# Block sums moved from GpSimd to VectorE, and every engine's steps ordered by one written table

## The chip, the core and the metric

The kernel runs on one core of a Trainium2 chip. The core has a matrix unit (TensorE: PE, its weight loads PEld), VectorE (DVE), ScalarE (ACT), GpSimd (POOL), and SyncE (SP), which here only issues DMA transfers. Each engine works through its own list of instructions in order; semaphores tie the lists together, so an instruction that waits holds up all that stands behind it on its engine. The metric is device time in microseconds (us); lower is better.

## What is computed

A decayed linear attention (2 batches, 8 heads, 768 positions, 64 features) feeds two expert layers with 1536 tokens, width 512 and inner width 2048:

```
for t in range(S):
    state = gamma * state + outer(k[t], v[t])        # per batch and head
    y[t] = scale * q[t] @ state
x = y as (1536, 512)
h = x @ moe_w_in;   x = elu(h) @ moe_w_out           # first layer
h = x @ moe2_w_in;  out = softplus(h) @ moe2_w_out   # second layer
```

The weights arrive as 64-bit floats. They are put together on chip from their two 32-bit halves. Products are made at higher than single-pass precision: each operand is split into a high and a low part, and three products (high·high, high·low, low·high) are added.

## The kernel before

**Stages.** The first stage runs attention (12 tiles of 128 positions) beside the first layer. The layer is worked in 48 units: 3 blocks of 512 tokens by 16 slices of the inner width. For unit u, `H.u` (`hidden`, L432, 12 matmuls) makes the hidden values, `aa`/`ab` apply the activation, `gh`/`gl` split it into high and low parts, and `R.u` (`project`, L470, 12 matmuls) adds into four output banks. `ih`/`il` and `oh`/`ol` split the two weight tiles of the unit. The third block of tokens is units 32 to 47.

The second stage is the second layer as 16 "quads": 2 groups of 768 tokens by 8 slices of the inner width. Its first product uses a scheme with seven block products (`multiply`, L613, numbers 1 to 7 of `products`, 6 matmuls each) in place of eight, at the price of sums and differences of operand blocks. For the weights these are `combine_w` (L544, four GpSimd operations on 128x256 in a quad of the first group, three in one of the second). For the tokens they are `combine_x` (L522, four GpSimd operations on 128x768 per group). `block_h/l` (L564, L567), `sum_h/l` (L575, L578), `operand_h/l` (L527, L532) and `out_h/l` (L582, L586) split the results. Products 1, 6, 7, 4 accumulate in one bank and 2, 5, 3 in another. ScalarE copies the partial results out of the first bank (`keep`, L620) before the next product may enter it. `gather` (L632, on VectorE, or L630 on ScalarE), `negate` (L636), `soften` (L640), `join` (L644), `gate_h` (L650) and `gate_l` (L654) make the gated values, and `project2` (L670, four times 9 matmuls per quad) multiplies them by the second weights.

**Weight conversion.** 64 weight tiles are loaded, 512 KB each, into four rotating `raw` buffers (L188, on SP's queue; for the first 32 loads every fifth goes to a spare buffer). A tile is converted by two ScalarE operations (L197, L198) and two VectorE operations (L210, L211). The second layer's tiles overwrite those of the first, and so can be converted only when the third block of tokens has used them.

**What sets the order.** The pools and semaphores are fixed, and the order in which the program calls its steps is the order on each engine. Three things make that order: `OPENING`, a written list of steps for the first third; `regular()`, a rule that goes on from there to the last units; and `quad()`, which gives every step of the second stage a due time, by which all are sorted. At the end of the first stage `regular()` has left several tiles of the second layer unconverted, and `quad()` puts two conversions into each of the first quads:

```python
        for n, (a1, b1) in enumerate(((3.8, 4.5), (9.9, 11.0))):
            if todo:
                i = todo.pop(0)
                at(t + a1, conv_a, i)
                at(t + b1, conv_b, i)
```

The tokens' operands of the second group are made at the end of the first group, by steps with due times from the start of the last quad of the first group on.

Of the kernel before, what the change touches and what calls it, by code (L numbers as in the profile page):

```python
# [11 lines left out]
F32 = mybir.dt.float32  # L12
F32R = mybir.dt.float32r
# [25 lines left out]
def tile_retention_elu_softplus(  # L39
# [134 lines left out]
    raws = {}  # L174
    parts = {}
    wide64 = w_in1.dtype != F32

    def load_w(i):
# [3 lines left out]
        if not wide64:  # L182
            nc.sync.dma_start(out=wf[f][o], in_=src)
            return
        spare = i < 2 * NF and i % 5 == 4
# [104 lines left out]
    def transposed(n, j):  # L290
        if j in blocked:
# [4 lines left out]
            if n == 0:  # L296
                nc.gpsimd.tensor_tensor(out=tf, in0=tf, in1=gq[j >= CPB], op=ALU.mult)
# [10 lines left out]
        elif j in plain:  # L308
# [3 lines left out]
        qkT[n, j] = t  # L312

# [6 lines left out]
    def state(j):  # L320
# [6 lines left out]
        else:  # L327
            tag = f"h{1 - max(hb) % 2}"
# [90 lines left out]
    hb = {}  # L419
    gs_ = {}  # L420
# [3 lines left out]
    def hidden(u):  # L424
# [31 lines left out]
    def project(u):  # L456
        layer, blk, f = units[u]
        oh, ol = ws.pop((u, 1))
        gh, gl = gs_.pop(u)
        fresh = f == 0  # L460
        if fresh:
            for i in range(4):
                acc[i] = psum(f"a{i}")
# [4 lines left out]
        for p, i in order:  # L468
# [19 lines left out]
    def finish(u):  # L488
        _, blk, f = units[u]
        if f != NF - 1:  # L490
            return
        for i in range(4):
            t = blk * TB
            parts = []
            while t < (blk + 1) * TB:
                e = min((blk + 1) * TB, (t // HT + 1) * HT)
                parts.append((t, e))
                t = e
            for n, (t, e) in enumerate(sorted(parts, key=lambda x: x[0] - x[1])):
                h = t // HT  # L500
                dst = yhalf(h // 2, h % 2)[:, i, t - h * HT:e - h * HT]
                src = acc[i][:, t - blk * TB:e - blk * TB]
                if n == 0:
                    nc.scalar.activation(out=dst, in_=src, func=AF.Copy)
                else:
                    nc.vector.tensor_copy(dst, src)
# [6 lines left out]
    source = (0, 2, 0, 0, 1, 2, 3)  # L513
# [453 lines left out]
```

## Time and profile before

| | us |
|---|---|
| median of 3 runs | 598.24 (597.95 to 600.91) |
| profiled execution, its own time | 596.96 |
| its span, first to last instruction | 595.2 |
| PE busy | 574.4 (97%) |
| VectorE busy | 458.9 (77%) |
| ScalarE busy | 377.3 (63%) |
| GpSimd busy | 100.8 (17%) |

PE's busy time is not PE at its peak, since matmuls overlap and their ends are modelled. The spacing from one matmul's start to the next says more. Of the other engines only the moments matter in which PE waits for them.

### The profile page before, as it was taken

Reading aid. Unit: us, or ns where it says so; the run is one execution under the profiler, and the core shown is the slowest. Engines: PE = TensorE matmul, PEld = TensorE weight load, DVE = VectorE, ACT = ScalarE, POOL = GpSimd, SP = SyncE. Lnnn points to the kernel's source line nnn. Section 1 sums busy time; section 2 is a strip of 40 time slices with the busy share of each in tenths; the row PEclk is TensorE's granted clock in tenths of the full one; section 3 lists DMA queues with packets and bytes.
Section 4 is the critical chain, followed back from the end, with each engine's and each line's share of the span. In section 5 each row is a group of like instructions: output and inputs, shape, how many; then the busy total and the mean of one; then the engine's idle time right before and its main releaser. Section 6 shows DMA issues by size and latency. Waiting matters only on the chain.

```text
span 595.2 us, 8756 instructions
## 1 busy us (share of the span) xinstructions
PE 574.4 (97%) x3236; PEld 487.5 (82%) x3236; DVE 458.9 (77%) x729; ACT 377.3 (63%) x678; POOL 100.8 (17%) x101
## 2 busy tenths in 40 slices
PE   8999899999999999999999799999996999999996
PEld 5888688888888888888888688889885999889995
DVE  3899899976555647899998798888789876766653
ACT  2596887946454456987997666666664655555542
POOL 3310200010010000215002222222225111111000
PEclk9999999999999999999999799999998999999999
DMA  9985958753220002233434122200000200000002
GB/s 198 275 272 158 259 171 210 196 134 60 38 47 9 1 1 72 71 107 106 143 108 140 35 72 71 72 0 2 1 0 1 107 1 1 1 0 2 1 0 106
DMA packets 75835, 48.30 MB, mean 81 GB/s; under 512 B 53520, under 2 KB 69904, under 8 KB 75792
## 3 DMA queue, kind: packets, MB, share of 16 engines
q1 hardware_dynamic: 75216, 46.94, 28.7%
q10 hardware_dynamic: 576, 0.80, 0.4%
q8 instruction: 25, 0.41, 0.3%
q14 instruction: 18, 0.15, 0.1%
HBM read 44.58 MB, written 3.15 MB: 80 GB/s over the span
## 4 chain that ended last, share of the span: by engine, by line
PE 70%; DVE 13%; issue 7%; ACT 4%; SPq 4%; DMA 2%; POOL 1%; ACTq 0%; DVEq 0%; POOLq 0%
PE psb L470 21%; PE psb L432 19%; PE psb L670 14%; PE psb L613 13%; SPq L97 3%; DVE cl L210 2%; DVE wo L586 2%; DMA v<-v 1%; DVE hx L632 1%; DVE g L654 1%; DVE hx L644 1%; PE psb L353 1%; DVE wo L211 1%; DVE op L532 1%; ACT g L650 1%
## 5 line engine op out<-in xcount | busy, mean ns | idle before, releaser
L670 PE MATMUL psb<-wo,g 128*128 128x512 f32 x576 | 142.9, 393 | 0.0
L670 PEld LDWEIGHTS psb<-wo,g 128*128 128x128 f32 x576 | 108.2, 189 | 19.6
L432 PE MATMUL psb<-x,wh 128*128 128x512 f32 x384 | 95.9, 391 | 0.0
L432 PEld LDWEIGHTS psb<-x,wh 128*128 128x128 f32 x384 | 71.5, 188 | 15.2 <-issue 0.3
L544 POOL TENSOR_TENSOR y<-wi 128x256 f32<-128x256 f32 x48 | 49.6, 1053 | 196.5 <-DVE wx L578 117.8
L613 PE MATMUL psb<-op,wx 128*128 128x384 f32 x336 | 68.7, 344 | 3.4 <-DVE hx L632 2.3
L613 PEld LDWEIGHTS psb<-op,wx 128*128 128x128 f32 x336 | 61.3, 192 | 7.0 <-DVE hx L632 2.8
L640 ACT ACTIVATE hx<-hx 128x384 f32<-128x384 f32 x64 | 33.6, 524 | 44.6 <-DVE hx L636 44.5
L470 PE MATMUL psb<-gh,wh 128*128 128x512 f32 x192 | 56.0, 398 | 0.0
L470 PE MATMUL psb<-gh,wl 128*128 128x512 f32 x192 | 54.4, 390 | 0.0
L470 PE MATMUL psb<-gl,wh 128*128 128x512 f32 x192 | 54.3, 389 | 0.0
L210 DVE SCALAR_TENSOR_TENSOR cl<-cm,cl 128x512 int32<-128x512 int32 x64 | 48.6, 759 | 5.3 <-ACT cl L198 5.3
L650 ACT ACTIVATE g<-hx 128x384 fp32r<-128x384 f32 x64 | 33.4, 523 | 29.9 <-DVE hx L644 29.9
L432 PE MATMUL psb<-x,wl 128*128 128x512 f32 x192 | 51.3, 389 | 0.0
L654 DVE TENSOR_TENSOR g<-hx,g 128x384 fp32r<-128x384 f32 x64 | 37.1, 581 | 16.7 <-ACT g L650 16.4
L439 ACT ACTIVATE e<-psb 128x512 f32<-128x512 f32 x48 | 28.4, 592 | 32.4 <-PE psb L432 31.3
L224 DVE TENSOR_TENSOR wl<-wo,wh 128x512 fp32r<-128x512 f32 x48 | 35.0, 729 | 17.9 <-ACT wh L218 17.8
L644 DVE SCALAR_TENSOR_TENSOR hx<-hx 128x384 f32<-128x384 f32 x64 | 37.3, 584 | 14.7 <-ACT hx L640 12.9
L197 ACT ACTIVATE cm<-raw 128x512 f32<-128x512 f32 x64 | 42.4, 662 | 7.7 <-DMA raw<-moe_w_out 3.7
L613 PE MATMUL psb<-op,wa 128*128 128x384 f32 x192 | 39.8, 349 | 6.5 <-ACT hx L630 2.4
L444 DVE SCALAR_TENSOR_TENSOR e<-e,psb 128x512 f32<-128x512 f32 x48 | 32.6, 680 | 16.8 <-ACT e L440 16.8
L613 PEld LDWEIGHTS psb<-op,wa 128*128 128x128 f32 x192 | 34.9, 193 | 10.4 <-ACT hx L630 4.1
(98 smaller groups left out, 933.1 us busy)
## 6 DMA issues: line engine op xcount, KB each, us to landing
raw<-moe_w_in SPq DMA_DIRECT2D x32, 512.0 KB, 4.0
raw<-moe_w_out SPq DMA_DIRECT2D x32, 512.0 KB, 3.6
out_dram<-o SPq DMA_DIRECT2D x9, 256.0 KB, 2.4
early<-q SPq DMA_DIRECT2D x4, 256.0 KB, 4.9
early<-k SPq DMA_DIRECT2D x4, 256.0 KB, 5.1
early_v<-v SPq DMA_DIRECT2D x4, 256.0 KB, 5.0
qb<-q SPq DMA_DIRECT2D x64, 16.0 KB, 2.2
qb<-k SPq DMA_DIRECT2D x64, 16.0 KB, 1.9
```

The lines of the kernel that those rows point to most:

```text
L197: nc.scalar.activation(out=m, in_=r[:, :, :, 1].bitcast(F32), func=AF.Copy, scale=2.0 ** -112)
L210: nc.vector.scalar_tensor_tensor(out=l, in0=m.bitcast(I32), scalar=3, in1=l, op0=ALU.logical_shift_left, op1=ALU.bitwise_or)
L224: nc.vector.tensor_tensor(out=l, in0=wf[f][o], in1=ws[u, o][0].bitcast(F32), op=ALU.subtract)
L432: nc.tensor.matmul(b, w[:, kk, :], x[:, kk, :], start=(n == 0), stop=(n == len(seq) - 1))
L470: nc.tensor.matmul(acc[i], st[:, i * P:(i + 1) * P], mv, start=(fresh and p == 0), stop=(f == NF - 1 and p == 2))
L544: nc.gpsimd.tensor_tensor(out=out, in0=x, in1=y, op=o)
L613: nc.tensor.matmul(bank_p[b], w[:, h, k], x[:, l, k], start=(start and i == 0), stop=(i == len(seq) - 1), skip_group_check=True)
L640: nc.scalar.activation(out=e, in_=e, func=AF.Softplus)
L644: nc.vector.scalar_tensor_tensor(out=e, in0=h, scalar=0.0, in1=e, op0=ALU.max, op1=ALU.add)
L650: nc.scalar.activation(out=t[:, 0], in_=hid[Q, c][1], func=AF.Copy)
L654: nc.vector.tensor_tensor(out=t[:, 1], in0=hid.pop((Q, c))[1], in1=t[:, 0].bitcast(F32), op=ALU.subtract)
L670: nc.tensor.matmul(sums2[s], t[:, x, i * P:(i + 1) * P], o[:, w], start=(left[s] == 0 and p == 0), stop=(left[s] == 2 * NQ - 1 and p == 2) ...
```

## The change

`combine_w` and `combine_x` run on VectorE. In the second group two of the three weight sums become one operation on 128x512. A spare tile `t2` takes one of the four token differences, so that it overwrites nothing. The operands 0 and 1 of the second group go into the `raw` buffers, which are free by then, and can so be made while the first group still uses its own. Conversion is cut into four steps (`ct`, `cl` on ScalarE, `cj`, `cs` on VectorE), the activation into `ar` and `ae`, the copies of the first layer's result into eight steps `F`, and `project` can be called for part of its matmuls. `OPENING`, `regular()` and `quad()` are gone: `TABLE` lists every step. The number of matmuls does not change. Output tiles come from `tmp` rather than `raw`, and all but one are sent from SP's queue.

```diff
-    def combine_x(n):
-        g, n = divmod(n, 8)
-        d, a, b = ((0, 1, 0), (1, 3, 1), (0, 3, 0), (2, 2, 0))[n]
-        nc.gpsimd.tensor_tensor(out=quarter(g, d), in0=quarter(g, a), in1=quarter(g, b), op=ALU.subtract)
+        second["t2"] = second["op"].tile([P, KK // 2 * HT], F32, name="t2")
+
+    def combine_x(g, n):
+        d, a, b = ((0, 1, 0), (1, 3, 1), (4, 3, 0), (2, 2, 4))[n]
+        nc.vector.tensor_tensor(out=place(g, d), in0=place(g, a), in1=place(g, b), op=ALU.subtract)
+
+    def operand_h(g, n):
+        if g and n < 2:
+            t = [raw.tile([P, 4 * 2 * P], F32R, tag="raw", name=f"op{n}")[:, :KK // 2 * HT] for i in range(2)]
...
-    def combine_w(Q):
+    def combine_w(Q, n):
         a, s = quads(Q), sums()
-
-        def op(out, x, y, o):
-            nc.gpsimd.tensor_tensor(out=out, in0=x, in1=y, op=o)
-
         if Q < NQ:
...
+            out, x, y = ((s[:, 0], a[:, 2], a[:, 3]), (s[:, 2], a[:, 0], a[:, 2]), (a[:, 2], s[:, 0], a[:, 0]),
+                         (s[:, 1], a[:, 1], a[:, 2]))[n]
+        elif n < 2:
+            out, x, y = ((s[:, 0], a[:, 2], a[:, 0]),
+                         (s[:, 1:3], a[:, 1::2], a[:, 2:3].to_broadcast([P, 2, KH])))[n]
...
+        nc.vector.tensor_tensor(out=out, in0=x, in1=y, op=ALU.subtract if n else ALU.add)
...
-PAUSE = {7: 2, 8: 1, 9: 1, 10: 1}
-OPENING = """
...
+TABLE = """
...
+gl.39 ct.46 cs.44 R.38 ar.40 cj.45 Lw.48 ih.42 cs.45 ae.40 il.42 cl.46 Lw.49 ab.40 ct.47 H.41 oh.40 cj.46 gh.40 ol.40 cl.47
+gl.40 ct.48 cj.47 R.39 cs.46 ar.41 cs.47 ih.43 Lw.50 ae.41 Lw.51 il.43 cl.48 ab.41 ct.49 cj.48 H.42 gh.41 cs.48 oh.41 cl.49
...
+    for t in TABLE.split():
+        name, *args = t.split(".")
+        steps[name](*map(int, args))
```

Three places show how instructions move. Line numbers are those of the kernel that each list belongs to. The first is ScalarE's list where the two stages meet. Before, from the second `keep` of quad 0 (first row) to the third `keep` (seventh row):

```order
L620 ACTIVATE hx<-psb 128x384
L504 ACTIVATE y_2620<-psb 128x384 x4
L650 ACTIVATE g_3458<-hx 128x384
L575 ACTIVATE wb<-y_2620 128x768
L197 ACTIVATE cm<-raw 128x512
L198 ACTIVATE cl<-raw 128x512
L620 ACTIVATE hx<-psb 128x384
L582 ACTIVATE wo_3469<-wo_124 128x512
```

After, from the same second `keep` (L703 is `keep`, L585 the copy of the first layer's result, L658 `sum_h`, L665 `out_h`, L731 `gate_h`):

```order
L703 ACTIVATE hx<-psb 128x384
L585 ACTIVATE y_2565<-psb 128x384 x3
L703 ACTIVATE hx<-psb 128x384
L665 ACTIVATE wo_3538<-wo_124 128x512
L731 ACTIVATE g_3548<-hx 128x384
L658 ACTIVATE wb<-y_2565 128x768
```

The third `keep` now stands behind three copies; four other operations that stood ahead of it, among them a conversion, are gone or stand behind it.

The second place is VectorE's list there. Before, from the first `gate_l` (L654) to the `gather` of the second column (L632):

```order
L654 TENSOR_TENSOR g_3458<-hx,g_3458 128x384
L578 TENSOR_TENSOR wb<-y_2620,wb 128x768
L586 TENSOR_TENSOR wo_3469<-wo_124,wo_3469 128x512
L210 SCALAR_TENSOR_TENSOR cl<-cm,cl 128x512
L211 SCALAR_TENSOR_TENSOR wo_133<-raw,cl 128x512
L632 TENSOR_TENSOR hx<-psb,hx 128x384
L636 TENSOR_SCALAR hx<-hx 128x384
```

After (L293 is the last conversion step, L587 the copies of the first layer's result, L713 `gather`, L669 `out_l`, L735 `gate_l`):

```order
L293 SCALAR_TENSOR_TENSOR wo_139<-raw,cl 128x512
L587 COPY y_2565<-psb 128x128 x4
L713 TENSOR_TENSOR hx<-psb,hx 128x384
L669 TENSOR_TENSOR wo_3538<-wo_124,wo_3538 128x512
L735 TENSOR_TENSOR g_3548<-hx,g_3548 128x384
```

The `gather` now stands ahead of `out_l` and `gate_l`, and the last conversion of the whole program ahead of the copies.

The third place is the meeting of the two groups. Before, GpSimd had these block sums there (L544 weights, L522 tokens):

```order
L544 TENSOR_TENSOR y_2620<-wi_116 128x256 x3
L522 TENSOR_TENSOR y_2620<-y_2620 128x768 x3
L544 TENSOR_TENSOR y_2620<-wi_117 128x256 x3
L522 TENSOR_TENSOR y_2620<-y_2620 128x768
L544 TENSOR_TENSOR y_2620<-wi_118 128x256 x3
```

After, these are rows of VectorE, much earlier, among the gating steps of quads 1 and 2 (L637 `combine_w`, L606 `combine_x`, L619 `operand_l` of the second group):

```order
L637 TENSOR_TENSOR wi_120<-y_2565,wi_120 128x256
L619 TENSOR_TENSOR op_3619<-y_2565,op_3618 128x768
L669 TENSOR_TENSOR wo_3788<-wo_129,wo_3788 128x512
L637 TENSOR_TENSOR y_2565<-wi_120 128x256
L713 TENSOR_TENSOR hx<-psb,hx 128x384
L606 TENSOR_TENSOR y_2565<-y_2565 128x768
L717 TENSOR_SCALAR hx<-hx 128x384
L606 TENSOR_TENSOR t_2391<-y_2565 128x768
```

The token differences of the second group and its first two operands have moved some five quads forward and to another engine; GpSimd has nothing left in the second stage.

## Rows read from the trace of the kernel before

**Rows 1.** Waits of the matrix unit: us in total, times, longest.

```profile
PE psb L390 <- POOL wide L318: 2.4, 1, 2.4
```

**Rows 2.** Matrix unit in order of time, where the stages meet: start, us, what.

```profile
326.43 1.21 PE L613 MATMUL psb<-op,wx 128*128 128x384 f32 x6
329.81 1.99 PE L613 MATMUL psb<-op,wa 128*128 128x384 f32 x6 [2.17 <-ACT hx L620]
334.08 4.76 PE L613 MATMUL psb<-op,wx 128*128 128x384 f32 x18 [2.29 <-DVE hx L632]
338.68 2.23 PE L670 MATMUL psb<-wo,g 128*128 128x512 f32 x9
```

**Rows 3.** The chain that ended last: start, us, what.

```profile
308.73 2.72 PE psb L470 x12
...
344.00 1.14 DVE wa L567
...
409.93 1.13 DVE wa L567
...
466.46 2.07 PE psb L670 x9
...
560.60 2.07 PE psb L670 x9
562.67 2.11 PE psb L613 x12
```

**Rows 4.** Matrix unit in order of time, where the groups meet.

```profile
445.58 1.22 PE L613 MATMUL psb<-op,wx 128*128 128x384 f32 x6
448.19 1.33 PE L613 MATMUL psb<-op,wb 128*128 128x384 f32 x6 [1.40 <-DVE hx L632]
449.35 2.25 PE L670 MATMUL psb<-wo,g 128*128 128x512 f32 x9
452.99 1.32 PE L613 MATMUL psb<-op,wa 128*128 128x384 f32 x6 [1.39 <-ACT hx L630]
456.29 2.14 PE L613 MATMUL psb<-op,wa 128*128 128x384 f32 x6 [1.98 <-DVE hx L632]
458.23 3.01 PE L670 MATMUL psb<-wo,g 128*128 128x512 f32 x9
```

**Rows 5.** VectorE in order of time, where the groups meet.

```profile
430.38 0.56 DVE L644 SCALAR_TENSOR_TENSOR hx<-hx 128x384 f32<-128x384 f32 x1 [0.59 <-ACT hx L640]
...
438.72 1.87 DVE L644 SCALAR_TENSOR_TENSOR hx<-hx 128x384 f32<-128x384 f32 x1 [0.46 <-ACT hx L640]
```

**Rows 6.** VectorE in order of time, where the stages meet.

```profile
311.87 0.68 DVE L210 SCALAR_TENSOR_TENSOR cl<-cm,cl 128x512 int32<-128x512 int32 x1
312.59 0.69 DVE L211 SCALAR_TENSOR_TENSOR wi<-raw,cl 128x512 int32<-128x512 int32 x1
313.20 0.69 DVE L224 TENSOR_TENSOR wl<-wo,wh 128x512 fp32r<-128x512 f32 x1
313.80 0.69 DVE L453 TENSOR_TENSOR gl<-e,gh 128x512 fp32r<-128x512 f32 x1
...
331.22 1.21 DVE L210 SCALAR_TENSOR_TENSOR cl<-cm,cl 128x512 int32<-128x512 int32 x1
```

**Rows 7.** Busy time by stretch: PE, PEld, DVE, ACT, POOL, clock, DMA share, GB/s.

```profile
229.00:316.00 87.00, 87.00 (x385) 72.06 (x384) 77.69 (x112) 72.88 (x129) 13.00 (x8) 1.00 0.35 113
...
344.00:418.00 74.00, 72.19 (x353) 63.48 (x351) 64.45 (x103) 46.48 (x88) 20.61 (x20) 1.00 0.14 43
```

**Rows 8.** Groups by line: busy us, mean ns.

```profile
L345 DVE TENSOR_TENSOR st<-st,dec 128x256 f32<-128x256 f32 x8 | 3.4, 424 | 0.3
```

**Rows 9.** Conversion operation L198 by stretch: ACT busy (count), clock, DMA share, GB/s.

```profile
60.00:75.00 15.00, 3.94 (x6) 1.00 0.91 262
...
300.00:315.00 15.00, 2.67 (x4) 1.00 0.44 140
```

**Rows 10.** DMA issues by tile: KB each, median us to landing.

```profile
raw<-moe_w_in SPq DMA_DIRECT2D x32, 512.0 KB, 4.0
```

More of the change, by code (lines that the diff above doesn't have):

```diff
@@ L181, in load_w @@
         src = src[f * P:(f + 1) * P, :] if o else src[:, f * P:(f + 1) * P].rearrange("(k p) f -> p k f", p=P)
[L182 to L185, printed above, removed]
+        spare = len(loaded) < 2 * NF and len(loaded) % 5 == 4
+        loaded.append(i)
         r = (ap if spare else raw).tile([P, 4, P, 2], I32, tag="raw", name="raw")
@@ L327, in state @@
         else:
-            tag = f"h{1 - max(hb) % 2}"
+            tag = f"h{1 - last[0] % 2}"
             b = bank["s", j] = psum(tag)
@@ L419, in tile_retention_elu_softplus @@
     hb = {}
+    last = [0]
     gs_ = {}
@@ L467, in project @@
             order = [(p, i) for i in range(4) for p in range(3)]
-        for p, i in order:
+        for p, i in order[a:e]:
             st, mv = passes[p]
@@ L486, in yhalf, with finish @@
         return ytile(g)[:, n * KK * HT:(n + 1) * KK * HT].rearrange("p (k t) -> p k t", k=KK)
[L488 to L506, printed above, removed]
+    def finish(u, i, n):
+        blk = units[u][1]
+        a = blk * TB
+        m = (a // HT + 1) * HT
+        t, e = sorted(((a, m), (m, a + TB)), key=lambda x: x[0] - x[1])[n]
+        h = t // HT
+        dst = yhalf(h // 2, h % 2)[:, i, t - h * HT:e - h * HT]
+        src = acc[i][:, t - a:e - a]
+        if n == 0:
+            nc.scalar.activation(out=dst, in_=src, func=AF.Copy)
+        else:
+            nc.vector.tensor_copy(dst, src)
     def quarter(g, n):
@@ L512, in tile_retention_elu_softplus, with place @@
     second = {}
-    source = (0, 2, 0, 0, 1, 2, 3)
+    source = (0, 2, 4, 0, 1, 2, 3)
+    def place(g, n):
+        return second["t2"] if n == 4 else quarter(g, n)
     def close_attention():
@@ L673, in project2 @@
             seen2[g, s] = left[s] + 1
+    outs = {}
     def store(g, s):
-        o = raw.tile([P, 2 * DM], F32, tag="raw", name="o")[:, :DM]
+        o = outs[g, s] = tmp.tile([P, DM], F32, tag=("cm", "cl")[s % 2], name="o")
         if s % 2:
@@ L922, in tile_retention_elu_softplus @@
-    for _, _, fn, args in sorted(plan, key=lambda x: x[:2]):
-        fn(*args)
+        "H": hidden, "ar": act_r, "ae": act_e, "ab": act_b, "gh": act_h, "gl": act_l, "R": project, "F": finish,
+        "kc": keep_clock, "few": few_banks, "end": close_attention,
+        "xt": combine_x, "yh": operand_h, "yl": operand_l, "cw": combine_w, "bh": block_h, "bl": block_l, "sh": sum_h,
+        "sl": sum_l, "wh": out_h, "wl": out_l, "op": open_products, "cf": close_first, "M": multiply, "u": keep, "c": gather,
```

404 lines of the change are left out of this document (133 added, 271 removed).

## The prediction

> **What bounds the kernel now.** I read the busy times first, and then the matrix unit (PE) in order of time against its own pace. Undisturbed, 12 matmuls of a first-layer unit step take 2.72 us, 12 of a block product pair 2.11 and 9 of a projection 2.07 [rows 3], so one matmul costs 0.227, 0.176 and 0.230 us, and one unit (`H` and `R`) 5.44 us. Over the third block of tokens PE has no wait at all: busy 87.00 of 87 us [rows 7]. So PE bounds the kernel, and only what PE loses to others can be won without fewer matmuls. It loses time in four places.
>
> Where the stages meet, from 326.43 to 338.68 us (12.25 us) PE runs 6+6+18 block product matmuls [rows 2], worth 30 × 0.176 = 5.3 us. It loses 7.0 us. The waits name ScalarE's `keep` (L620) and VectorE's `gather` (L632).
>
> Where the groups meet, from 445.58 to 458.23 (12.65 us) it runs 24 block product and 9 projection matmuls [rows 4], worth 4.2 + 2.1 = 6.3 us, and loses 6.4 us. The nine matmuls that follow take 3.01 us where the same nine took 2.25 at 449.35, another 0.8. Together 7.1 us.
>
> In the first quads one step of VectorE (L567) starts at 344.00 and, four quads on, at 409.93 [rows 3]: 16.48 us a quad. Late in the kernel the same projection starts at 466.46 and six quads on at 560.60: 15.69. Each of four quads loses 0.79, 3.2 us in all.
>
> In the opening PE waits once for GpSimd's spreading of the attention state, 2.4 us [rows 1].
>
> These make 7.0 + 7.1 + 3.2 + 2.4 = 19.7 us, the most that a better order can win without touching the matmuls, the start or the tail.
>
> **The change part by part.** GpSimd's block sums. While GpSimd works on SBUF, VectorE's instructions grow: the conversion step L210 takes 0.68 us at 311.87 and 1.21 at 331.22 [rows 6], and `join` (L644) takes 0.56 at 430.38 and 1.87 at 438.72, where the token differences run [rows 5]. The two long stalls of PE sit in such stretches. With GpSimd idle in the second stage all of that stretching goes. What comes in is four operations on 128x256 in a quad of the first group, and one on 128x256 plus one on 128x512 in the second. The same shape from SBUF takes 0.42 us [rows 8], a 128x512 one starts 0.60 after its neighbour [rows 6]: 1.7 and about 1.0 us a quad, and 0.9 us (an estimate by columns from the same rows) for each of eight token differences. In a converting quad VectorE was busy 64.45 of 74 us, 87% [rows 7], its conversions included. Those go, so no quad gets fuller by the sums alone.
>
> Conversions. By the order, 12 stand on VectorE behind the first `gather` before, and none after quad 0 now. They go into the third block of tokens, where the table joins 26 tiles over the eleven units from `H.37` to the first product, 59.8 us of PE. VectorE has there 44 split and activation operations and 51 conversion operations (26 joins, 25 signs). At 0.605 us from start to start, as the back-to-back rows stand [rows 6], these are 57.5 us; at their full 0.69 us, 65.6. So VectorE is between 2 us under PE and 6 over. I take 1.5 us lost, near the spacing, because the table puts other work between the two dependent conversion steps, and because VectorE was busy 77.69 of 87 us in this block [rows 7] while PE lost nothing.
>
> Where the stages meet, PE's own order is nearly the old one: `R.47` is only cut into 9 and 3 matmuls, with a block product between. What moved is ahead of it. The third `keep` stood behind four copies, a gate, a sum and a conversion on ScalarE, and now stands behind three copies; the `gather` stood behind a conversion on VectorE and now does not. `keep` can start when product 7 ends, and the three matmuls of `R.47` cover it (0.68 us). I keep back 0.7 us; the bounds are 0 and the 2.2 us that the wait has now [rows 2].
>
> Quads 1 and 2 take the token differences and two operands of the second group. By the order a quad of the first group holds 15 gating steps on 384 columns (at most 0.48 us each by columns, an estimate from the 0.60 for 512 [rows 6]; four of them are lighter, so some 6.5), `block_l` 1.14 [rows 3], one more sum of 768 columns 0.9, two weight splits 1.2 and the block sums 1.4 to 1.7: 11.3. Quad 2 adds three token differences and two operands of 768 columns, 0.9 each: 15.8 of PE's 15.69, and quad 1 about as much, since the last column of quad 0 falls into it. Bounds: 0, and twice what a converting quad loses now, 2 × 1.6 = 3.2 us. I take 1.0. This is the steepest load of the second stage; from quad 3 on it is 13 us and less.
>
> Where the groups meet nothing runs on GpSimd, and the operands 0 and 1 are there long before; 2 to 6 are made as their tiles come free. I keep back 0.8 us; the bounds are 0 and one wait of 1.4 [rows 4].
>
> The opening. The value tile of attention step 5 and its decay come ahead of their old place, so the 2.4 us wait should go. The price is on SP's queue: five attention and decay loads, 1.25 MB, now stand ahead of the weight loads 4 to 6, which at 262 GB/s [rows 9] land up to 4.8 us later. They are needed about two units later, which covers it; I take 0, with bounds of -1 and +4.8.
>
> The output's tiles and queues change, but each tile is still held by its transfer in the same way; I take 0.
>
> Sum: 596.96 (the profiled execution's own time) - 19.7 + 1.5 + 0.7 + 1.0 + 0.8 = 581.3. The median of the runs shown is 1.3 us above that execution: 582.5.
>
> One rule speaks against the change. VectorE is the fuller engine here, 89% in the third block, and PE loses nothing beside it [rows 7]; by that row the added work is free until VectorE passes PE. The Trainium skill (Perfetto Trace Analysis, Optimizing Scalar/DVE Operations) says that a saturated VectorE may hand work to ScalarE or even GpSimd, though between GpSimd and VectorE, which share a port, it might not help. The change does the reverse. By that rule the end would be the first rival's; the stretched rows bear out its second half instead, and by them it is my forecast's.
>
> **The rivals.** *VectorE becomes the bound.* In the third block it takes 6 us more than PE (the upper end above), quads 1 and 2 lose 3.2, and the two meetings 2.2 + 1.4, instead of the 4.0 that I keep back: 12.8, so 591.3. For it: VectorE at 95% and more for some 90 us, with chains over three engines in which each handover costs. Against it: in the third block it was already 89% full, stretched by GpSimd, at no loss. Half of it gives 587.
>
> *The conversions become the bound, and the kernel is slower.* All loads of the third block go through four buffers. A load lands after 4.0 us [rows 10], then four conversion steps have to run before the buffer is free. The table wants one tile every 59.8 / 26 = 2.3 us. The fastest pace in the trace is 6 in 15 us, 2.5 us each, in the opening with a fifth buffer; in the third block it is 4 in 15 us, 3.75 each [rows 9]. Every tile that is late holds ScalarE and VectorE, whose lists are in order, and so `H` and `R`. At 2.5 us it costs 26 × 0.2 = 5 us, at 3.75 it costs 38: 616. It decides from 26 × 0.76 = 19.7 us on, a pace of 3.06. Against it: the DMA share is 0.44 at the slow pace [rows 9], so the loads waited for the old order, not for the queue; and four buffers at 2.3 us leave 9.2 us for 4.0 of landing and 2.6 of four steps.
>
> *The waits only move.* The stalls at the two meetings come from the long chain through the seven products, not from GpSimd and the conversions, and stay in about their size; the early wins are paid back in the third block. Then the time is 595 to 599. Against it: the rows name late `keep`s and `gather`s, which stand behind stretched work.
>
> **How the numbers follow.** My forecast (577 to 588.5) gets 0.64, VectorE as the bound (to 594) 0.18, the moved waits 0.08, the slow conversions 0.07, and something better than 577 (the opening also gains) 0.03. About 0.5%, 3 us, is what a measurement can tell. Faster: 0.64 + 0.18 + 0.03 = 0.85; same 0.08; slower 0.07. The lower end is 598.2 - 19.7 - 1 = 577.5, put at 577; the upper end takes in most of the first rival, 593.
>
> **What would show it.** Right: PE's waits between 310 and 345 us and where the groups meet are under 1.5 us each; quads 1 to 4 run at 15.7 us; L210's successor takes 0.68 throughout the third block; there are no GpSimd rows in the second stage; units 37 to 47 run at 5.44 us. Wrong: units of the third block at 5.6 us and more with PE waiting for `gh`, `gl` or the split weights; ScalarE's first conversion step waiting for a DMA of `raw`; quads 1 and 2 over 16 us; new waits of PE in the opening for weights.

## The result and the profile after

The changed kernel takes 584.82 us (median of 4 runs, 583.69 to 585.43) beside 598.75 us (597.95 to 600.91, 4 runs) for the kernel before: a ratio of 0.976, 95% interval 0.973 to 0.979. It is faster by 2.4%, and 2.3 us behind the forecast of 582.5. The profiled execution took 584.83 us, its span is 583.1 us, 12.1 us shorter than before.

The page's busy times: PE falls from 574.4 to 570.0 us, GpSimd from 100.8 to 28.4 us.

```profile
PE 570.0 (98%) x3236; PEld 485.5 (83%) x3236; DVE 451.5 (77%) x785; ACT 371.7 (64%) x678; POOL 28.4 (5%) x37
```

VectorE took over the sums, and its busy time still fell from 458.9 to 451.5 us. The move between the engines does not give that by itself: in the runs below VectorE is busy 460.2 us with the sums on VectorE in the old order (`sums_vector`), and 450.4 us with the sums on GpSimd in the new one (`sums_gpsimd`). The waits of the matrix unit, as in [rows 1] (total us, times, longest):

```profile
PE psb L517 <- DVE st L428: 3.6, 1, 3.6
PE psb L517 <- ACT x L495: 1.9, 1, 1.9
PE psb L240 <- DVE warm L234: 1.3, 1, 1.3
PE psb L480 <- DVE A L447: 0.8, 2, 0.6
PE psb L417 <- POOL early_v L363: 0.6, 1, 0.6
PE psb L370 <- DVE early L360: 0.5, 1, 0.5
```

The wait for `wide` is gone, and so is every wait of the block products (now L696). In their place stand two others, both before the first-layer unit step `hidden` (now L517). Busy time by stretch, as in [rows 7]: the third block, the meeting of the stages, then quads 1 and 2 (PE, PEld, DVE, ACT, POOL, clock, DMA share, GB/s).

```profile
226.00:313.00 87.00, 87.00 (x386) 72.06 (x385) 81.47 (x132) 75.80 (x138) 0.00 (x0) 1.00 0.48 151
313.00:342.00 29.00, 29.00 (x143) 25.72 (x142) 26.12 (x52) 25.11 (x47) 0.00 (x0) 1.00 0.18 57
345.00:360.00 15.00, 15.00 (x76) 13.51 (x75) 14.85 (x30) 9.47 (x18) 0.00 (x0) 1.00 0.00 1
360.00:375.00 15.00, 15.00 (x76) 13.51 (x75) 14.61 (x29) 7.98 (x16) 0.00 (x0) 1.00 0.00 0
```

PE is busy throughout in all four. VectorE is 94% full in the third block and 97 to 99% in quads 1 and 2, and holds nothing up. Where the stages meet, PE in order of time, as in [rows 2]:

```profile
331.24 1.23 PE L696 MATMUL psb<-op,wx 128*128 128x384 f32 x6
...
333.04 1.31 PE L696 MATMUL psb<-op,wa 128*128 128x384 f32 x6
334.19 3.34 PE L696 MATMUL psb<-op,wx 128*128 128x384 f32 x18
337.37 2.24 PE L751 MATMUL psb<-wo,g 128*128 128x512 f32 x9
```

The same 30 block product matmuls, with three of the last `project` between them, now take 6.1 us (331.24 to 337.37) instead of 12.25, and no row has a wait.

Waits name places but not sums, so I cut both traces at the same matmuls: the first of units 0, 16 and 32, then the first block product of quads 0, 1, 5 and 9, and the end of the span. The numbers are the distances between these starts, in us; the runs below will be read in the same table. One trace stands for each run, and traces whose steps are the same in a stretch still differ by up to 0.6 us where the stages meet (`late_conv`, `late_tiles`, `best`), and by almost 2 us before unit 16 and in block 2 (`after`, `late_ops`, `sums_gpsimd`).

| | to unit 0 | block 1 (units 0 to 15) | block 2 (16 to 31) | block 3 (32 to 47) | stages meet (quad 0) | quads 1 to 4 | groups meet (5 to 8) | rest |
|---|---|---|---|---|---|---|---|---|
| before | 27.9 | 102.7 | 99.1 | 87.0 | 19.4 | 65.6 | 70.7 | 122.7 |
| after | 29.1 | 100.1 | 106.0 | 87.0 | 13.0 | 62.8 | 62.7 | 122.4 |
| sums_vector | 26.3 | 102.9 | 99.1 | 87.0 | 19.8 | 66.4 | 67.7 | 123.2 |
| conv_early | 27.8 | 103.4 | 99.1 | 92.8 | 17.7 | 64.3 | 69.9 | 122.5 |
| conv_early_vector | 26.4 | 104.6 | 99.1 | 90.6 | 22.0 | 64.6 | 66.0 | 123.0 |
| sums_gpsimd | 28.3 | 102.3 | 104.4 | 87.0 | 13.5 | 63.3 | 62.7 | 122.0 |
| late_ops | 28.3 | 100.9 | 104.1 | 87.0 | 13.0 | 62.8 | 65.3 | 122.4 |
| late_conv | 28.6 | 100.3 | 99.4 | 87.0 | 13.0 | 62.7 | 62.7 | 122.4 |
| both | 27.6 | 103.6 | 103.8 | 87.0 | 13.0 | 62.7 | 62.7 | 122.4 |
| late_tiles | 29.0 | 101.8 | 99.1 | 87.0 | 13.6 | 62.7 | 62.7 | 122.4 |
| tiles_gpsimd | 29.0 | 100.6 | 99.1 | 87.0 | 13.9 | 63.3 | 62.7 | 122.0 |
| tiles_late_ops | 29.0 | 100.2 | 99.1 | 87.0 | 13.0 | 62.7 | 65.3 | 122.4 |
| best | 27.6 | 102.1 | 99.1 | 87.0 | 13.0 | 62.7 | 62.7 | 122.4 |
| glued | 29.0 | 100.4 | 99.1 | 87.0 | 17.8 | 62.7 | 62.7 | 122.4 |

From before to after: the meetings and quads give back 6.4 + 2.9 + 8.0 = 17.3 us, the end 0.3; unit 16 starts 1.4 us earlier; and block 2, where nothing was lost before, takes 6.9 us more. Together 12.1 us. Two things need an explanation: what gave the 17.3 us, and what costs 6.9 us in block 2.

The second can be followed row by row. SP issues the block loads of the last attention tiles (`qb`, 16 KB each, 0.47 us from one to the next) without a break, and then four weight loads. The last of the four lands at 161.85 us, by the chain of work that ended last (third row, with its start and length).

```profile
144.78 7.49 SPq L204 DMA_DIRECT2D qb<-k  x16
152.36 2.04 SPq L269 DMA_DIRECT2D raw<-moe_w_in  x4
...
153.94 7.91 DMA raw<-moe_w_in
```

These four are the second layer's tiles 32 to 35. The table has their first conversion steps in ScalarE's list at units 19 to 21, long before anyone needs them. ScalarE:

```profile
156.70 0.66 ACT L274 ACTIVATE cm<-raw 128x512 f32<-128x512 f32 x1 [4.26 <-DMA raw<-moe_w_in]
...
161.93 0.66 ACT L274 ACTIVATE cm<-raw 128x512 f32<-128x512 f32 x1 [0.86 <-DMA raw<-moe_w_in]
162.50 0.58 ACT L525 ACTIVATE e<-psb 128x512 f32<-128x512 f32 x1
162.98 0.62 ACT L300 ACTIVATE wh<-wi 128x512 fp32r<-128x512 f32 x1
```

Behind the last of them stand the activation (L525) and the weight split (L300) of the running unit. VectorE waits for that split, with the attention state (L428) in its list behind it:

```profile
163.63 0.69 DVE L306 TENSOR_TENSOR wl<-wi,wh 128x512 fp32r<-128x512 f32 x1 [2.24 <-ACT wh L300]
164.24 0.68 DVE L532 SCALAR_TENSOR_TENSOR e<-e,psb 128x512 f32<-128x512 f32 x1
164.84 0.70 DVE L377 STREAM_TRANSPOSE qT<-qb 128x512 f32<-128x512 f32 x1
165.47 0.39 DVE L428 TENSOR_TENSOR st<-psb,st 128x256 f32<-128x256 f32 x1
```

And the matrix unit's next `hidden` needs the bank that the state step empties:

```profile
161.31 1.07 PE L558 MATMUL psb<-gl,wh 128*128 128x512 f32 x4
166.00 3.75 PE L517 MATMUL psb<-x,wh 128*128 128x512 f32 x8 [3.62 <-DVE st L428]
169.55 1.91 PE L517 MATMUL psb<-x,wl 128*128 128x512 f32 x4
171.26 1.43 PE L558 MATMUL psb<-gh,wh 128*128 128x512 f32 x4
172.53 1.07 PE L558 MATMUL psb<-gh,wl 128*128 128x512 f32 x4
```

From 161.31 to 172.53 PE runs 20 matmuls, worth 20 × 0.227 = 4.5 us, in 11.2: 6.7 us are lost, 3.8 of them idle and 2.9 at half pace. Eight matmuls take 3.75 us where they take 1.98 elsewhere, and over 166 to 171 us the granted clock is 0.50: after the idle time it stood at 1.2 instead of 2.4 GHz.

### The profile page after: what moved, and what is told of

Its sections match the earlier page's. It is cut to its first block, busy times and chain, and to the rows that moved or that the text cites. A ratio compares the mean times of both kernels' runs of the same rounds, so it can differ in the third digit from the quotient of the medians.

```text
span 583.1 us, 8690 instructions
## 1 busy us (share of the span) xinstructions
PE 570.0 (98%) x3236; PEld 485.5 (83%) x3236; DVE 451.5 (77%) x785; ACT 371.7 (64%) x678; POOL 28.4 (5%) x37
## 4 chain that ended last, share of the span: by engine, by line
PE 91%; SPq 3%; DMA 3%; ACT 1%; DVE 1%; issue 0%; DVEq 0%; ACTq 0%
PE psb L517 23%; PE psb L751 22%; PE psb L558 22%; PE psb L696 20%; DMA raw<-moe_w_in 3%; SPq L180 2%; PE psb L437 1%; SPq L269 1%; PE psb L466 1%; PE psb L370 0%; PE psb L417 0%; PE psb L459 0%; PE psb L480 0%; DMA out_dram<-o 0%; PE psb L474 0%
## 5 line engine op out<-in xcount | busy, mean ns | idle before, releaser
L517 PE MATMUL psb<-x,wh 128*128 128x512 f32 x384 | 97.8, 397 | 5.6 <-DVE st L428 3.6
L517 PEld LDWEIGHTS psb<-x,wh 128*128 128x128 f32 x384 | 72.4, 191 | 22.0 <-ACT gh L536 4.0
L696 PE MATMUL psb<-op,wx 128*128 128x384 f32 x336 | 67.0, 339 | 0.0
L696 PEld LDWEIGHTS psb<-op,wx 128*128 128x128 f32 x336 | 60.2, 188 | 2.5
L306 DVE TENSOR_TENSOR wl<-wi,wh 128x512 fp32r<-128x512 f32 x48 | 33.7, 701 | 33.6 <-ACT wh L300 33.6
L517 PE MATMUL psb<-x,wl 128*128 128x512 f32 x192 | 52.2, 394 | 0.0
L284 DVE SCALAR_TENSOR_TENSOR cl<-cm,cl 128x512 int32<-128x512 int32 x64 | 45.2, 710 | 8.4 <-ACT cl L279 8.4
L525 ACT ACTIVATE e<-psb 128x512 f32<-128x512 f32 x48 | 28.4, 592 | 34.4 <-PE psb L517 34.3
L536 ACT ACTIVATE gh<-e 128x512 fp32r<-128x512 f32 x48 | 30.2, 629 | 24.3 <-DVE e L532 24.3
L731 ACT ACTIVATE g<-hx 128x384 fp32r<-128x384 f32 x64 | 33.2, 520 | 18.7 <-DVE hx L725 18.6
L669 DVE TENSOR_TENSOR wo<-wo,wo 128x512 fp32r<-128x512 f32 x32 | 22.0, 687 | 29.7 <-ACT wo L665 29.7
L517 PEld LDWEIGHTS psb<-x,wl 128*128 128x128 f32 x192 | 36.6, 191 | 7.8
L279 ACT ACTIVATE cl<-raw 128x512 int32<-128x512 uint32 x64 | 42.5, 665 | 0.6 <-DVE wo L293 0.5
L558 PEld LDWEIGHTS psb<-gh,wl 128*128 128x128 f32 x192 | 36.1, 188 | 7.7
L558 PEld LDWEIGHTS psb<-gl,wh 128*128 128x128 f32 x192 | 36.0, 188 | 7.5
```

The costliest lines, as they stand in the source:

```text
L279: nc.scalar.activation(out=l, in_=raws[i][:, :, :, 0].bitcast(U32), func=AF.Copy, scale=2.0 ** -29 * (1 - 2.0 ** -12), bias=-0.499)
L306: nc.vector.tensor_tensor(out=l, in0=wf[f][o], in1=ws[u, o][0].bitcast(F32), op=ALU.subtract)
L517: nc.tensor.matmul(b, w[:, kk, :], x[:, kk, :], start=(n == 0), stop=(n == len(seq) - 1))
L536: nc.scalar.activation(out=gh, in_=acts[u], func=AF.Copy)
L558: nc.tensor.matmul(acc[i], st[:, i * P:(i + 1) * P], mv, start=(fresh and p == 0), stop=(f == NF - 1 and p == 2))
L696: nc.tensor.matmul(bank_p[b], w[:, h, k], x[l][:, k], start=(start and i == 0), stop=(i == len(seq) - 1), skip_group_check=True)
```

## The experiments

All times are medians; each ratio is to the kernel before as it ran beside that run, with a 95% interval.

**The wait in block 2: `late_conv`.** The eight conversion steps of tiles 32 to 35 move behind `R.20`, two units later. (The table's names: `Lw` weight load, `m` attention mask, `tk`, `tq`, `gt` VectorE's transposes and decay of an attention tile, the rest as in the sections above.)

```diff
-il.21 ct.32 m.9 cl.32 ab.19 ct.33 tk.11 cl.33 H.20 oh.19 cj.32 gh.19 cj.33 ct.34 ol.19 gl.19 O.9 ct.35 ar.20
+il.21 m.9 ab.19 tk.11 H.20 oh.19 gh.19 ol.19 gl.19 O.9 ar.20
...
-ol.21 R.20 ar.22
+ol.21 R.20 ct.32 cl.32 ct.33 cl.33 cj.32 cj.33 ct.34 ct.35 ar.22
```

> Table as in the changed kernel, but the eight conversion steps of tiles 32 to 35 that stand among units 19 to 21 are moved two units later, behind R.20. Theory (ScalarE's list is held by these conversions, whose loads SP issued only at 152.4 us, behind its block loads): the 3.6 us wait of PE and the half clock behind it go, 6.3 us: 578.5. Rival (the wait is for the transposes of the attention tile and GpSimd's decay, whose small loads are late): the wait stays, 584 to 585.

Measured: 578.02 us (577.84 to 584.22), ratio 0.969 (0.963 to 0.975). Block 2 takes 99.4 us, the wait for the state is gone from PE's list, and the rest of the table's row is within 0.5 us of the changed kernel's. So the wait cost what its rows say: 6.8 us of the median. Three of the four runs are within 0.4 us of each other, and one is at 584.22; with that one the interval still touches the changed kernel's (0.973 to 0.979), while that of `late_tiles` below does not.

**The opening as well: `both`.** In the opening ScalarE's first `hidden` operand (`xh.3`, L495) stands behind a conversion whose load comes late:

```profile
27.36 0.66 ACT L274 ACTIVATE cm<-raw 128x512 f32<-128x512 f32 x1 [1.66 <-DMA raw<-moe_w_in]
27.92 0.65 ACT L279 ACTIVATE cl<-raw 128x512 int32<-128x512 uint32 x1
28.47 0.59 ACT L495 ACTIVATE x<-psb 128x512 fp32r<-128x512 f32 x1
```

`both` is `late_conv` with the two ScalarE steps of tile 2 behind `xh.3`.

```diff
-cj.1 Lw.5 ct.2 cs.1 cl.2 few ST.3 xh.3 Lw.6
+cj.1 Lw.5 cs.1 few ST.3 xh.3 ct.2 cl.2 Lw.6
```

> As the run with the later conversions, and in the opening the two ScalarE steps of conversion 2 stand behind the high part of the tokens of tile 3 (xh.3). Theory: the 2.1 us wait in the opening goes as well: 576.5 (575.5 to 577.5). Rival (the weight load is late for the first units anyway, so the wait moves to H.1 or H.2): 578 to 579.

Measured: 582.49 us (579.79 to 584.54), ratio 0.974 (0.969 to 0.979): worse than `late_conv`, and neither expectation had that. Unit 0 starts at 27.6, but unit 16 no earlier (131.1), and block 2 loses 4.7 us by another wait of the same kind. VectorE:

```profile
132.24 0.68 DVE L305 TENSOR_TENSOR wl<-wo,wh 128x512 fp32r<-128x512 f32 x1
138.16 0.71 DVE L376 STREAM_TRANSPOSE kT<-qb 128x512 f32<-128x512 f32 x1 [5.23 <-DMA qb<-k]
```

The transpose of attention tile 9 (`tk.9`) waits for its last block load, and everything behind it on VectorE with it. SP issued those 16 loads from 127.74 us on, where it was 123.99 in `late_conv`. So a shift of 3.7 us in SP's queue is enough to make that transpose wait. Why SP's queue was later here is not shown. The lone 584 us of `late_conv` may be the same thing; there is no trace of it.

**The transposes too: `late_tiles`.** `late_conv` with the transposes of tiles 9 and 10 one or two units later.

```diff
-ae.13 tk.9 Lk.9 il.15
+ae.13 Lk.9 il.15
...
-gl.14 Lb.83
+gl.14 tk.9 Lb.83
...
-ih.18 tk.10 ae.16 il.18 Lb.89 ab.16 ST.8 xh.8 tq.10 gh.16 R.14 Lb.90 xl.8 gt.10 st.8
+ih.18 ae.16 il.18 Lb.89 ab.16 ST.8 xh.8 gh.16 R.14 Lb.90 xl.8 st.8
...
-R.16 ol.17 ar.18
+R.16 ol.17 tk.10 tq.10 gt.10 ar.18
```

> As the run with the later conversions, and the transposes of attention tiles 9 and 10 and the decay of tile 10 one to two units later, so that VectorE no longer stands behind SP's block loads. Theory (in the second block SP issues its loads without a break, and every transpose that comes before its load holds VectorE): 577 to 578, no wait of PE on VectorE's state step anywhere, and less spread than the run with the later conversions. Rival (the loads are not the limit there): same as that run with the same spread.

Measured: 579.32 us (577.96 to 580.49), ratio 0.969 (0.967 to 0.971). No run is far out, and no wait of PE for the transposes of the last attention tiles or for the state is left. The median is above the 577 to 578 us of the theory.

**The opening again: `best`.** `late_tiles` with the steps `ct.2` and `cl.2` behind `xh.3` and VectorE's `cj.2` behind `xl.3`, the operands of unit 0.

```diff
-cj.1 Lw.5 ct.2 cs.1 cl.2 few ST.3 xh.3 Lw.6 dv.4 cj.2 ih.1 xl.3
+cj.1 Lw.5 cs.1 few ST.3 xh.3 ct.2 cl.2 Lw.6 dv.4 ih.1 xl.3 cj.2
```

> The run with the later tiles, and conversion 2 behind the tokens of tile 3 on both engines: its two ScalarE steps behind xh.3 and its first VectorE step behind xl.3. Theory (in the earlier run with two edits only ScalarE's half was moved, so that the low part xl.3 still stood behind the conversion on VectorE): the opening's wait of some 2 us goes: 576.5 to 578. Rival (the weights land too late for H.1 and H.2 anyway): no faster than the run with the later tiles.

Measured: 578.49 us (577.61 to 578.76), ratio 0.967 (0.965 to 0.970), the lowest upper end of all, but not apart from `late_tiles`, as the rival had it. Unit 0 starts 1.4 us earlier than there, unit 16 1.1 us: over the fourteen traces of the table unit 0 starts between 26.3 and 29.1 and unit 16 between 128.9 and 131.2, old order and new.

**The engine alone, in the old order: `sums_vector`.** The kernel before, with only the engine of the sums changed.

```diff
-        nc.gpsimd.tensor_tensor(out=quarter(g, d), in0=quarter(g, a), in1=quarter(g, b), op=ALU.subtract)
+        nc.vector.tensor_tensor(out=quarter(g, d), in0=quarter(g, a), in1=quarter(g, b), op=ALU.subtract)
...
-            nc.gpsimd.tensor_tensor(out=out, in0=x, in1=y, op=o)
+            nc.vector.tensor_tensor(out=out, in0=x, in1=y, op=o)
```

> The kernel before, with its old order, and the block sums of weights and tokens on VectorE: the move between engines alone. Theory (the order does most; the engine move removes the stretching but puts the same work into the same late places of VectorE): 591 to 597, the two meetings still losing 3 to 6 us each. Rival (GpSimd's interference is the whole loss): 581 to 585, as the changed kernel. A third: slower than before, over 601, since VectorE gets more work exactly where PE waits for it.

Measured: 595.67 us (594.16 to 597.87, 10 runs), ratio 0.9957 (0.9935 to 0.9979), within the theory's range. Where the stages meet nothing is won (19.8 us for 19.4), and the waits are those of [rows 2], with GpSimd idle:

```profile
328.39 2.03 PE L613 MATMUL psb<-op,wa 128*128 128x384 f32 x6 [2.17 <-ACT hx L620]
333.02 6.10 PE L613 MATMUL psb<-op,wx 128*128 128x384 f32 x18 [2.60 <-DVE hx L632]
```

The stretching is gone there, but the four weight sums now stand in VectorE's list ahead of that `gather`, so this run alone can't price the stretching; `sums_gpsimd` below can. Where the groups meet it wins 3.0 us.

**The order alone: `sums_gpsimd`.** The changed kernel, its table untouched, with the sums back on GpSimd (`nc.vector` for `nc.gpsimd` in the two lines of `combine_x` and `combine_w`, the other way round).

```diff
-        nc.vector.tensor_tensor(out=place(g, d), in0=place(g, a), in1=place(g, b), op=ALU.subtract)
+        nc.gpsimd.tensor_tensor(out=place(g, d), in0=place(g, a), in1=place(g, b), op=ALU.subtract)
```

> The changed kernel's table, with the block sums back on GpSimd. Theory (interference matters in quads where VectorE is nearly full): quads 1 and 2 and the third block's end lose, 588 to 595. Rival (with a good order GpSimd does as well): 583 to 586.

Measured: 585.85 us (585.28 to 587.17), ratio 0.980 (0.976 to 0.984), 1.0 us above the changed kernel, with overlapping intervals: the rival's time, 2 us under the theory's. Where the stages meet it takes 13.5 us, with GpSimd at work. So the order does nearly all of it without the engine. Since block 2 disturbs both, the pair was run once more in the mended table.

**The same in the mended order: `tiles_gpsimd`.** `late_tiles` with the sums on GpSimd.

> The run with the later tiles, with the block sums on GpSimd: what the engine is worth once no load holds the second block. Theory from the run with the old engine in the new table: 1 us, 580 to 581. Rival (the loads' waits hid the engine's share there): 583 or more.

Measured: 578.60 us (578.12 to 579.30), ratio 0.968 (0.965 to 0.971): not apart from `late_tiles`, and below what either expectation had. The stretch of [rows 5, 6] is there. VectorE where the stages meet:

```profile
319.66 0.96 DVE L305 TENSOR_TENSOR wl<-wo,wh 128x512 fp32r<-128x512 f32 x1 [0.51 <-ACT wh L299]
320.55 1.22 DVE L540 TENSOR_TENSOR gl<-e,gh 128x512 fp32r<-128x512 f32 x1
```

In `late_tiles` both take 0.68 to 0.69. Quad 0 takes 13.9 us beside 13.6 in `late_tiles` and 13.0 in `best`, so 0.3 to 0.9 us more; quads 1 to 4 take 0.6 us more, and what follows the meeting of the groups 0.4 us less without the sums on VectorE. The Trainium skill (SBUF — State Buffer, SBUF: two separate sides) says that a VectorE operation with two SBUF inputs and a GpSimd operation that reads SBUF lock the shared ports against each other, the first for its whole instruction, while the other is blocked; the longer rows agree that they collide, by 0.28 and 0.54 us. The Trainium skill (Perfetto Trace Analysis, Optimizing Scalar/DVE Operations) says that moving work between the two might not help; the trace agrees: 0.5 to 1.1 us of the stages above in all, and no difference in the medians.

**The early operands: `late_ops` and `tiles_late_ops`.** The changed kernel, and `late_tiles`, with the second group's token differences and its first two operands moved from quads 1 and 2 back to the end of quad 7, directly ahead of operand 2.

```diff
-M.1.6 yh.1.0 vl.0.2 vl.0.1 yh.1.1 M.1.5
+M.1.6 vl.0.2 vl.0.1 M.1.5
...
-c.2.2 xt.1.0 M.2.4 n.2.2 xt.1.2 s.2.2
+c.2.2 M.2.4 n.2.2 s.2.2
...
-u.1 vl.7.0 yh.1.2
+u.1 vl.7.0 yh.1.0 yh.1.1 yl.1.0 yl.1.1 xt.1.0 xt.1.2 xt.1.1 xt.1.3 yh.1.2
```

> The changed kernel with the first two operands and the four token differences of the second group made in the last quad of the first group, where the old order had them, still on VectorE. Theory (making them early is what removed the stall where the groups meet): VectorE gets 5.2 us more in a quad where it has 13 of 15.7, the meeting loses 3 to 5 us: 588 to 590. Rival (it was GpSimd's interference, and VectorE does it at any place): 584 to 586.

Measured: 588.94 us (585.53 to 590.08), ratio 0.986 (0.984 to 0.989), within the theory's range. The trace is of the fastest of the four runs; what makes the others 2.6 to 4.6 us longer is not shown.

> The run with the later tiles, with the second group's first two operands and four differences made in the last quad of the first group: what making them early is worth by itself. Theory: 2.6 us where the groups meet, 581.5 to 582.5. Rival (the 4 us between the medians before are all of it): 583 to 584.

Measured: 581.05 us (580.60 to 581.75), ratio 0.972 (0.968 to 0.976). That is just below both expectations. In both traces the groups' part is 2.6 us longer, 65.3 for 62.7; from quad 1 on no other part moves, and what moves ahead of it moves in other traces of these orders too. The second's median is 1.7 us above `late_tiles` and 2.6 us above `best`, which ran beside it. Its matrix unit has two waits there:

```profile
435.54 1.32 PE L695 MATMUL psb<-op,wx 128*128 128x384 f32 x6 [1.35 <-ACT hx L702]
437.57 1.33 PE L695 MATMUL psb<-op,wb 128*128 128x384 f32 x6 [0.71 <-DVE hx L712]
```

Quads 1 to 4, freed of that work, are no shorter (62.8 and 62.7 for 62.8 and 62.7): the early operands cost nothing there.

**Conversions early by the old rule: `conv_early`, `conv_early_vector`.** The kernel before, with two conversions in every unit of the third block, so that one is left for the second stage; the second run with the sums on VectorE as well.

```diff
-            if not last or u % 4 == 0:
-                cb()
+            cb()
...
-            if not last or u % 4 == 3:
-                ca()
+            ca()
```

> The kernel before with two conversions in every unit of the third block, so that one is left for the second stage, sums still on GpSimd. Theory (the conversions held the keep and the gather where the stages meet and made the quads 0.79 us longer): the four quads' 3.2 us and some 4 of the 7.0 us go: 590 to 593. Rival (the third block cannot take them: PE waits there): 597 to 603.

> The same with the block sums on VectorE. Theory (the two parts add up: 7 us by the conversions, 3 by the engine, and what is then missing to the changed kernel is the place of the second group's operands and the order where the stages meet): 587 to 590. Rival (with the conversions gone the engine is all: as the changed kernel): 584 to 586.

Measured: 599.61 us (597.51 to 602.68, 10 runs), ratio 1.0018 (0.9998 to 1.0038), which the rival had, and 597.63 us (595.00 to 599.46, 10 runs), ratio 0.998 (0.996 to 1.000), above both expectations of the second. What the quads win, the third block loses: 92.8 and 90.6 us for 87.0. The first one's matrix unit now waits there for ScalarE's conversion step and for the splits that stand behind it:

```profile
280.50 1.21 PE L470 MATMUL psb<-gl,wh 128*128 128x512 f32 x4 [0.35 <-DVE gl L453]
282.52 2.06 PE L432 MATMUL psb<-x,wh 128*128 128x512 f32 x8 [0.81 <-ACT cl L198]
...
288.45 2.08 PE L432 MATMUL psb<-x,wh 128*128 128x512 f32 x8 [0.17 <-ACT cl L198]
```

And the stages' meeting stays at 17.7 and 22.0 us. That is not a meeting without conversions, though. In `conv_early` the two that stood right ahead of the third `keep` and of the `gather` are gone, and PE's waits for them fall from 2.17 and 2.29 us [rows 2] to 1.05 and 0.40 (with 1.17 us for a later `gather`):

```profile
330.17 1.32 PE L613 MATMUL psb<-op,wx 128*128 128x384 f32 x6 [0.89 <-DVE hx L632]
...
337.74 1.31 PE L613 MATMUL psb<-op,wa 128*128 128x384 f32 x6 [1.05 <-ACT hx L620]
339.45 2.65 PE L613 MATMUL psb<-op,wx 128*128 128x384 f32 x12 [0.40 <-DVE hx L632]
```

But the conversions run late: VectorE starts three joins (L210) in quad 0, behind the first block product, in both runs, where the kernel before has two there and the changed kernel one, and new waits like the first row come ahead. In the third block the table's order has as many conversions (28 joins between the first matmul of unit 32 and the first block product, in `conv_early` 28 too), and there they cost nothing.

**Conversion steps glued: `glued`.** `late_tiles`, with the two ScalarE steps of tiles 36 to 63 next to each other again, and the two VectorE steps too. The first step of each pair comes later by that, so the run changes two things at once.

```diff
-gl.39 ct.46 cs.44 R.38 ar.40 cj.45 Lw.48 ih.42 cs.45
-ae.40 il.42 cl.46
+gl.39 cj.44 cs.44 R.38 ar.40 Lw.48 ih.42 cj.45 cs.45
+ae.40 il.42 ct.46 cl.46
```

> The mended table (574 to 581 us in its run: 579.3), with one change: for the tiles 36 to 63 the two ScalarE conversion steps stand next to each other again, and the two VectorE steps too, as they did in the kernel before; everything else keeps its place. Theory: the third block takes 26 conversions without a loss because the four steps are cut apart and each stands between other work, so that a late load or a dependent step holds up little; glued, the first step waits for its load later and the units 37 to 47 lose 1 to 5 us in all, so 580.5 to 584, and the matrix unit shows waits for the split weights or the gated values there. Rival: what matters is which unit a conversion stands in and how far behind its load, not whether its steps are apart; then the third block still shows the matrix unit busy 87 of 87 us and the time is 578.5 to 580.

Measured: 582.97 us (582.55 to 585.68), ratio 0.973 (0.970 to 0.977). Dearer, as the theory had it, but not where it said: PE is busy in the whole third block, and quad 0 takes 17.8 us instead of 13.6 (13.0 in `best`). The work piles up behind: three joins (L283) start after the first block product, as in `conv_early`, and in `late_tiles` one. The third block and the first 6 us of the meeting, from the start of unit 32 on, in `glued`:

```profile
228.46:315.46 87.00, 87.00 (x385) 72.06 (x384) 82.24 (x130) 76.24 (x138) 0.00 (x0) 1.00 0.52 156
315.46:321.46 6.00, 5.06 (x25) 4.16 (x24) 5.89 (x10) 5.55 (x10) 0.00 (x0) 1.00 0.32 104
```

The same in `late_tiles`:

```profile
229.91:316.91 87.00, 87.00 (x385) 72.07 (x384) 83.84 (x136) 77.53 (x141) 0.00 (x0) 1.00 0.52 164
316.91:322.91 6.00, 6.00 (x32) 5.45 (x32) 5.97 (x13) 4.66 (x9) 0.00 (x0) 1.00 0.01 3
```

When the first product starts, VectorE has done 130 instructions instead of 136, and is full. Its list in `glued` shows a part of why:

```profile
309.05 0.68 DVE L283 SCALAR_TENSOR_TENSOR cl<-cm,cl 128x512 int32<-128x512 int32 x1
309.76 0.69 DVE L292 SCALAR_TENSOR_TENSOR wo<-raw,cl 128x512 int32<-128x512 int32 x1
310.37 0.69 DVE L540 TENSOR_TENSOR gl<-e,gh 128x512 fp32r<-128x512 f32 x1
```

From the join to the sign that reads its result it is 0.71 us, and 0.61 from there to an instruction that doesn't need its result. In the 92 us from unit 32 on 27 of 28 joins in `glued` have their own sign directly behind them, 0.72 us each; in `late_tiles` 11 have. That is 16 × 0.11 = 1.8 us of the 4.2. The rest, the later first steps among it, I have no single row for; it shows as waits for an ever later VectorE (ScalarE waits 7.7 us for `ab`, L531, in that time, in `late_tiles` 1.7).

## Why the prediction came out as it did

**What held.** PE was the bound, and the losses were where three of the four places said (of the opening below): by the table the meetings and quads gave 17.3 us, where the sum had 7.0 + 7.1 + 3.2 - 0.7 - 0.8 - 1.0 = 14.8.

| step | predicted | measured |
|---|---|---|
| opening, up to unit 16 | -2.4 | -1.4 |
| block 2 | 0 | +6.9 |
| third block | +1.5 | 0.0 |
| stages meet | -6.3 | -6.4 |
| quads 1 to 4 | -2.2 | -2.9 |
| groups meet (quads 5 to 8) | -6.3 | -8.0 |
| rest | 0 | -0.3 |
| sum | -15.7 | -12.1 |

That the time came within 2.3 us of the forecast is partly luck: the 4.0 us kept back were not needed, and set off more than half of the 6.9 us that no term had. Of its signs of being right PE's waits, the quads at 15.7 us and the units 37 to 47 all came true; of its signs of being wrong one came as well, ScalarE's first conversion step waiting for a load of `raw`, but in block 2.

**The step that failed** is the one that took the opening and all behind it at 0 because later need "covers it": I priced the moved loads by their landing in the opening, and did not go on along SP's list to the loads behind the last block loads. That is my second rival's mechanism, a late tile that holds ScalarE's and VectorE's lists, in a block where I had not looked for it. It cost 6.9 us in the trace; `late_conv` removes it alone and is 6.8 us faster. Without it the kernel takes 578 to 579 us, near the lower end of the range.

**The 2.4 us of the opening** were counted as won when their wait goes. The wait went, and unit 0 started 1.2 us later, behind another late load (1.9 us for `xh.3`). By unit 16 the difference is -1.4 us, inside the spread of the traces of either order. The runs show no clear gain or loss there.

**The 4.0 us kept back** for a full VectorE were not needed. At 94 to 99% it held nothing up in this order. The bounds from the full duration (65.6 us for 59.8) were too high, and the 0.605 us spacing was nearer; it holds where dependent steps are apart. `glued` puts them together and later, and loses 4.2 us in quad 0, some 1.8 of it by the neighbourhood.

**The reason for the two meetings held only in part.** I put their stalls on GpSimd's stretching and on the conversions. The stretching is not what they wait for: without it, in the old order, the stages' meeting stays at 19.8 us (`sums_vector`), and with it, in the table's order, it takes 13.5 (`sums_gpsimd`; 13.9 in the mended table) beside 13.0. The conversions are not excluded. Moving them ahead by the old rule leaves 17.7 and 22.0 us, but three of them then run after the first block product; and in the table's own order, with three there instead of one (`glued`), the meeting takes 17.8. So it is the order that frees the meeting, and how much of that is the conversions' place is open. That its size came out (-6.4 us for -6.3) does not bear out the reason. Where the groups meet the engine is a part: 3.0 of 8.0 us in the old order, 2.6 by the early operands, and nothing by the engine in the new order. Of the four combinations (old order with GpSimd 598.75 and VectorE 595.67, new order 585.85 and 584.82) the order is worth 12.9 us with GpSimd and 10.9 with VectorE; the engine is worth some 3 us in the old order, and 1.0 us in the new, which is not clear of the noise.

Which single moves of the order free the stages' meeting was not tried: the later copies, the earlier `gather`, the moved gate and sum, and the place of the last conversions came only together. It is not settled either why unit 16 comes between 128.9 and 131.2 us from run to run.

## What to carry to other kernels

A wait that is removed is won only if the next thing that the engine needs is there: follow each in-order list on to the first instruction that waits for a load, above all a step that nobody needs yet, and put such a step behind everything that is urgent. Before moving work between engines, make the same order with the work where it is: here that gave nearly all of the gain. An engine that was full to 94 to 99% beside the bound cost nothing here in the one order, and 4.2 us in another with the same instructions; so look at what stands behind what, not at the busy share.

## What the runs showed of the hardware

- Small loads hold a queue's issuing engine: each 16 KB block load took 0.47 us of SP's list, so that 16 of them kept the weight loads behind waiting for 7.5 us, at a DMA share of 0.34 over 104 to 152 us. The last of the four weight loads then took 7.91 us to land.
- A PE idle time of 3.8 us cost another 2.9 us at the lower clock (granted 0.50 over 166 to 171 us), 8 matmuls in 3.75 us instead of 1.98.
- The second conversion step on VectorE, which reads the result of the one directly ahead, starts 0.71 to 0.73 us behind it on 128x512; an instruction that does not read it mostly 0.60 to 0.61.
- With GpSimd at work VectorE's operations on 128x512 grow from 0.68 to 0.96 and 1.22 us. In the mended order the total is not apart for that (578.60 us with GpSimd, 579.32 without); in the old order it is 0.4% lower with the sums on VectorE.
